# Q projection's last 64 rows in 32-row tiles, inside a 32-row transposition session

## The chip, the core and the metric

The kernel runs on one core of one Trainium2 chip. The metric is the device time of one execution in microseconds (us); the time shown for a kernel is the median of several runs. Engines are named as in the profile: PE (TensorE, matmuls; PEld are its weight loads), DVE (VectorE), ACT (ScalarE), POOL (GpSimd) and SP (SyncE, which issues nearly all DMAs here).

## The reference

Two independent attention blocks, A and B, of the same shape; their outputs are joined along the last axis. All arrays are bfloat16.

```python
# x (16, 80, 576); k_cache, v_cache (16, 16, 512, 128); wq (576, 4096); wo (4096, 576)
q = (x @ wq).reshape(16, 80, 32, 128).transpose(0, 2, 1, 3)
k = repeat(k_cache, 2, axis=1); v = repeat(v_cache, 2, axis=1)    # 16 kv heads, 32 q heads
p = softmax(einsum("bhqd,bhkd->bhqk", q, k) * 128 ** -0.5)
o = einsum("bhqk,bhkd->bhqd", p, v)
out = o.transpose(0, 2, 1, 3).reshape(16, 80, 4096) @ wo            # for A and for B
```

## The kernel before

**Units.** The work is cut into 128 units, 64 for A and then 64 for B. A unit is one batch and four kv heads, that is eight q heads. Each kv head has two q heads of 80 rows, 160 score rows: 128 of them fill one score tile (128 x 512), and the remaining 32 rows of the four kv heads make a fifth tile together. So a unit has five score tiles. Eight units (eight batches, the same heads) make an octet; Q is projected once for an octet.

**The steps of a unit, and their lines.**
- Q projection (L568). For each of the octet's eight heads, `em_qp` multiplies the head's 128 columns of wq by xT, over 576 contraction rows in five chunks of 128; the fifth chunk holds 64 rows of wq and 64 rows of zeros (set once by POOL, L400). It does so for the batches in two pieces, two batches (160 columns) and six batches (480 columns), each into one PSUM bank. `em_qev` evicts with the scale into `qT` (L579 on ACT, L580 on DVE).
- Scores. `em_qkr` (L672) makes the fifth tile of one or two units with four 32-column tiles of the array; `em_qk` (L686) makes each of the other four with one matmul of 512 columns.
- Softmax. DVE takes the negative row maximum (L695), ACT the exponential with the row sum (L699), DVE the reciprocal (L705), and POOL scales the probabilities in place (L708).
- Transposition (L741). `em_tr` turns the five scaled tiles into `pT`, with is-transpose matmuls against an identity. It uses 64-row tiles of the array, two at a time: 40 matmuls of 64 columns, into three banks. DVE copies two of the banks (L760, 1024 elements each), ACT or DVE the third (L758, L760).
- PV (L778): 16 matmuls of 160 columns, evicted to `oT` by ACT (L794).
- Output projection (L828): eight heads a step, 288 columns, over 16 heads; half of the sum waits in `acc` (L843), and the other half is added by DVE (L859) and stored.

```python
for n_ in range(20):                                                        # em_tr, before
    if n_ == 16:
        e.wait_ge(sems["e_tr"], U + 1)
    for h in range(2):
        ...
        last = e.matmul(dst, lhsT=p_sb[64 * h:64 * h + 64, psls[k_], j * 128:(j + 1) * 128],   # L741
                        rhs=ident[64 * h:64 * h + 64, 64 * h:64 * h + 64], start=True, stop=True,
                        is_transpose=True, tile_position=(64 * h, 0))
```

**Order.** Every operation is added to a list with a due time, a duration and the streams it belongs to. `_Sched.arrange` runs a planner over that list: it gives each operation its place on its engine, picks the PSUM bank among those that the operation's class allows (`BANKS`), and picks DVE or ACT where both are allowed. `finalize` then derives the semaphore waits from what each operation reads and writes. Each engine executes its list strictly in order. The planner treats score sessions of 32-column tiles (mode 1), transposition sessions (mode 2) and full-array matmuls (mode 0) as three modes and charges for a change between them.

**Loads.** SP loads K with a transposing DMA (five buffers) and V (four buffers), wq an octet at a time, wo in pieces, and for block B x with two transposing DMAs per half (512 rows, and 128 rows with the last 64). For block A, PE transposes x (L492).

## Time and profile before

| | |
|---|---|
| median of 3 runs | 739.65 us (738.3 to 740.1) |
| profiled execution | 739.38 us, its span 737.6 us |
| granted PE clock | 1.00 |
| POOL L708 | 640 instructions, 431.4 us busy |
| ACT L699 | 640, 443.1 us |
| DVE L695 | 640, 416.2 us |
| PE L568 / L778 / L686 / L828 / L741 | 1280 / 2048 / 512 / 1280 / 5120 matmuls |

"Busy" is the time in which an engine had at least one instruction under way; matmuls overlap, so that PE's busy time and the mean duration of a matmul say less than the distance from one start to the next. A line of the timeline gives the start in us, the time from the first start to the last end, the engine, the line of the kernel, the operation, what it writes and reads, and how many instructions were merged. "idle before" names what ended the wait.

### The profile page before, as it was taken

To read this page: it belongs to the slowest core of one execution; us is meant where nothing else is said; L and a number is where in the kernel's file an instruction comes from. 1 tells how busy PE (TensorE), PEld (TensorE's weight loads), DVE (VectorE), ACT (ScalarE), POOL (GpSimd) and SP (SyncE) were. 2 spreads that over 40 slices of the span, in tenths; PEclk is the share of its full clock that TensorE was granted. 3 is DMA by queue.
4 is the path that set the end of the run, shared out by engine and by line. 5 is a ranking of instruction groups with operands and counts; after the bars stand their busy time and mean duration, and the time that the engine had idled before them with its cause. 6 is when DMAs were issued, how large, how long until landed. Compare 5 with 4: busy or idle time off the path is not lost.

```text
span 737.6 us, 26159 instructions
## 1 busy us (share of the span) xinstructions
PE 730.7 (99%) x10818; PEld 510.8 (69%) x10818; DVE 650.3 (88%) x1344; ACT 625.7 (85%) x1827; POOL 433.8 (59%) x647
## 2 busy tenths in 40 slices
PE   9999999999999999999999999999999999999998
PEld 5566677677667676677677677666777677667776
DVE  4989999998999999888999999998889888998983
ACT  1889999999989889878889888989899888898881
POOL 1465666665666576556666565575565565665660
DMA  9999999999999999999999889999988978999920
GB/s 263 217 281 229 262 227 252 227 223 211 200 224 213 210 237 268 228 239 226 213 234 228 196 185 275 261 273 228 198 188 192 203 169 173 295 235 217 198 94 29
DMA packets 362102, 160.85 MB, mean 218 GB/s; under 512 B 276096, under 2 KB 358528, under 8 KB 361984
## 3 DMA queue, kind: packets, MB, share of 16 engines
q1 hardware_dynamic: 360768, 158.00, 97.3%
q8 instruction: 85, 1.39, 0.8%
q10 hardware_dynamic: 1216, 1.18, 0.5%
q14 instruction: 33, 0.27, 0.1%
HBM read 87.46 MB, written 2.95 MB: 123 GB/s over the span
## 4 chain that ended last, share of the span: by engine, by line
PE 96%; DVE 2%; ACT 1%; ACTq 0%; issue 0%
PE ps L568 23%; PE ps L828 21%; PE ps L778 19%; PE ps L686 15%; PE ps L741 12%; PE ps L672 5%; DVE negmax L695 1%; ACT p_sb L699 1%; PE ps L492 0%; DVE qT L580 0%; PE ps L429 0%; ACTq L545 0%; ACT oT L794 0%; ACT L448 0%; DVE pT L760 0%
## 5 line engine op out<-in xcount | busy, mean ns | idle before, releaser
L708 POOL TENSOR_SCALAR p_sb<-p_sb,rinv 128x512 bf16<-128x512 bf16 x640 | 431.4, 692 | 285.4 <-DVE rinv L705 283.5
L699 ACT ACTIVATE p_sb<-ps,negmax 128x512 bf16<-128x512 f32 x640 | 443.1, 701 | 27.8 <-DVE negmax L695 24.2
L695 DVE TENSOR_REDUCE negmax<-ps 128x1 f32<-128x512 f32 x640 | 416.2, 679 | 32.6 <-PE ps L672 16.8
L568 PE MATMUL ps<-xT,wq_sb 128*128 128x160 bf16 (+1 forms) x1280 | 206.0, 300 | 1.0 <-DVE xT L496 0.6
L778 PE MATMUL ps<-pT,v_sb 128*128 128x160 bf16 x2048 | 189.4, 233 | 0.0
L686 PE MATMUL ps<-kT,qT 128*128 128x512 bf16 x512 | 185.7, 380 | 0.0
L828 PE MATMUL ps<-wo_sb,oT 128*128 128x288 bf16 x1280 | 180.5, 286 | 0.0
L778 PEld LDWEIGHTS ps<-pT,v_sb 128*128 128x128 bf16 x2048 | 155.0, 98 | 35.1 <-DVE pT L760 0.6
L760 DVE COPY pT<-ps 128x1024 bf16<-128x1024 bf16 (+1 forms) x260 | 172.1, 676 | 6.0 <-PE ps L741 5.1
L568 PEld LDWEIGHTS ps<-xT,wq_sb 128*128 128x128 bf16 x1280 | 106.5, 98 | 66.1 <-issue 1.7
L828 PEld LDWEIGHTS ps<-wo_sb,oT 128*128 128x128 bf16 x1280 | 122.5, 98 | 40.6 <-issue 2.1
L699 ACT ACTIVATION_READ_ACCUMULATOR p_sb<-ps,negmax 128x1 f32 x640 | 137.5, 215 | 0.0
L794 ACT CAST oT<-ps 128x320 bf16<-128x320 f32 x256 | 108.7, 430 | 15.0 <-PE ps L778 14.1
L741 PEld LDWEIGHTS ps<-ident,p_sb 64*128 64x128 bf16 x5120 | 81.8, 95 | 37.9 <-issue 9.9
L741 PE MATMUL ps<-ident,p_sb 64*128 64x64 bf16 x5120 | 96.9, 190 | 0.0
L580 DVE TENSOR_SCALAR qT<-ps 128x480 bf16<-128x480 f32 (+1 forms) x131 | 65.2, 500 | 15.6 <-PE ps L568 14.7
L758 ACT COPY pT<-ps 128x256 f32<-128x256 f32 x124 | 47.3, 381 | 36.0 <-PE ps L741 35.4
L579 ACT ACTIVATE qT<-ps 128x160 bf16<-128x160 f32 (+1 forms) x125 | 52.8, 443 | 15.0 <-PE ps L568 14.3
L686 PEld LDWEIGHTS ps<-kT,qT 128*128 128x128 bf16 x512 | 49.6, 98 | 21.7 <-ACT p_sb L699 2.4
L705 DVE RECIPROCAL rinv<-rowsum 128x3 f32<-128x3 f32 (+1 forms) x256 | 41.2, 161 | 8.2 <-ACT p_sb L699 7.8
L672 PE MATMUL ps<-kT,qT 128*32 128x512 bf16 x512 | 39.6, 384 | 1.6 <-ACT p_sb L699 1.6
L859 DVE TENSOR_TENSOR osb<-ps,acc 128x288 bf16<-128x288 f32 x40 | 18.0, 451 | 16.1 <-PE ps L828 15.5
(25 smaller groups left out, 48.6 us busy)
## 6 DMA issues: line engine op xcount, KB each, us to landing
v_sb<-in_A_v_cache_dram SPq DMA_DIRECT2D x64, 512.0 KB, 4.8
v_sb<-in_B_v_cache_dram SPq DMA_DIRECT2D x64, 512.0 KB, 4.6
wo_sb<-in_A_wo_dram SPq DMA_DIRECT2D x8, 576.0 KB, 6.9
wo_sb<-in_B_wo_dram SPq DMA_DIRECT2D x8, 576.0 KB, 6.2
wq_sb<-in_B_wq_dram SPq DMA_DIRECT2D x4, 1024.0 KB, 7.1
out_dram<-osb SPq DMA_DIRECT2D x40, 72.0 KB, 3.7
wq_sb<-in_A_wq_dram SPq DMA_DIRECT2D x2, 1024.0 KB, 6.7
wq_sb<-in_A_wq_dram ACTq DMA_DIRECT2D x2, 512.0 KB, 6.9
```

The lines of the kernel that those rows point to most:

```text
L568: last = e.matmul(ps[:, vb.phys, 0:n1 - n0], lhsT=wq_sb[:, wsl, ck, i * 128:(i + 1) * 128], rhs=xT[:, half, ck, n0:n1], start=(ck == 0), s ...
L580: return e.tensor_scalar(dst, src, SCALE, None, op0=AluOpType.mult)
L672: last = e.matmul(ps[32 * g4:32 * g4 + 32, vb_.phys, :], lhsT=qT[:, qsl_, bl_, g4 * 160 + 128:g4 * 160 + 160], rhs=kT[:, ks_, :, g4 * 128: ...
L686: return e.matmul(ps[:, vb.phys, :], lhsT=qT[:, qsl, bl, gl * 160:gl * 160 + 128], rhs=kT[:, ks, :, gl * 128:(gl + 1) * 128], start=True, ...
L695: return e.tensor_reduce(negmax[:, si:si + 1], ps[:, vb.phys, :], axis=AX.X, op=AluOpType.max, negate=True)
L699: return e.activation(p_sb[:, psl, :], ps[:, vb.phys, :], AF.Exp, bias=negmax[:, si:si + 1], scale=1.0, accum_out=rowsum[:, ss, k:k + 1])
L708: return e.tensor_scalar(p_sb[:, psl, :], p_sb[:, psl, :], rinv[:, ss, k:k + 1], 1.0, op0=AluOpType.mult, op1=AluOpType.mult)
L741: last = e.matmul(dst, lhsT=p_sb[64 * h:64 * h + 64, psls[k_], j * 128:(j + 1) * 128], rhs=ident[64 * h:64 * h + 64, 64 * h:64 * h + 64], ...
L760: return e.tensor_copy(dst, src.rearrange("p (n c) -> p n c", n=16))
L778: last = e.matmul(ps[:, vo.phys, off:off + 160], lhsT=v_sb[:, vs, gl, j * 128:(j + 1) * 128], rhs=pT[:, pts, 4 * gl + j, :], start=(j == 0 ...
L794: return e.copy(dst, src)
L828: last = e.matmul(ps[:, vb.phys, 0:DC], lhsT=oT[:, hi, rb * 128:(rb + 1) * 128], rhs=wo_sb[:, wi, c3 * DC:(c3 + 1) * DC], start=(hi == 0), ...
```

## The change

**Q projection.** Work is cut into one piece per unit: two batches and four heads. Its first 512 rows are 16 full-array matmuls of 160 columns (four heads, four chunks). Each head has its own bank, and takes columns 320 to 479 of it. The last 64 rows become two rounds of four matmuls in 32-row tiles: round `h2` takes rows 32 `h2` to 32 `h2` + 31 for four heads at once, head r in the array's row group r. For that `wt` holds the last 64 rows of wq, 32 rows of each head on its own 32 partitions, and `xt` holds x's last 64 rows four times over. POOL makes the copies (`rep4`), and PE transposes them.

**Transposition.** 80 is-transpose matmuls of 32 columns in 32-row tiles, four at a time, into columns 0 to 319 (fp32) of the same four banks. Directly ahead of them, in the same session, come the eight tail matmuls of a later unit's Q. For 115 of the 128 pieces that is so; the 13 earliest have their tail among the other Q matmuls.

**Evictions.** The four banks are evicted two and two: DVE takes one pair, ACT the other (the table can swap them), with two copies each; the Q part follows (320 elements for two heads). PV evictions (`em_oev`) and the first half of the output projection (`em_ea`) may now be on either engine.

**Order.** The planner, its durations and `BANKS` go. `ORDER` is a string: each letter names a stream whose next operation is taken, an apostrophe ahead of it puts it on the other engine, and digits behind it are its banks.

**Sizes.** `NQ` (qT buffers) 3 to 2, `LA` (how far scores run ahead, in tiles) 10 to 11, `NS` (row maxima kept) 16 to 32; a small computation at the start (L439 to L451), whose result scales one accumulator copy (L841), goes. Wq of the first octet arrives in four pieces of 256 columns; the tail weights come in four loads for each set of eight heads.

```diff
@@ Q projection
-            for i in range(8):
-                for c in range(2):
...
-                        for ck in range(5):
-                            last = e.matmul(ps[:, vb.phys, 0:n1 - n0],
-                                            lhsT=wq_sb[:, wsl, ck, i * 128:(i + 1) * 128],
-                                            rhs=xT[:, half, ck, n0:n1], start=(ck == 0), stop=(ck == 4))
+            for m in range(8):
+                bp, hq = divmod(m, 2)
...
+                us = u0 - LQ + m
+                pre = us < US0
...
+                    def em_qp(e, h=h, hq=hq, wsl=wsl, half=half, n0=n0, vbq=vbq):
+                        for r in (2 * h, 2 * h + 1):
+                            for ck in range(4):
+                                last = e.matmul(ps[:, vbq[r].phys, QO:QO + 160],
+                                                lhsT=wq_sb[:, wsl, ck, (4 * hq + r) * 128:(4 * hq + r + 1) * 128],
+                                                rhs=xT[:, half, ck, n0:n0 + 160], start=(ck == 0), stop=False)
...
+                def em_qt(e, hq=hq, wsl=wsl, half=half, n0=n0, vbq=vbq):
+                    for h2 in range(2):
+                        for r in range(4):
+                            last = e.matmul(ps[:, vbq[r].phys, QO:QO + 160],
+                                            lhsT=wt[32 * r:32 * r + 32, wsl, h2, hq, :],
+                                            rhs=xt[32 * r:32 * r + 32, half, h2, n0:n0 + 160],
+                                            start=False, stop=(h2 == 1), tile_position=(32 * r, 0))
@@ transposition
-                    for h in range(2):
...
-                        last = e.matmul(dst, lhsT=p_sb[64 * h:64 * h + 64, psls[k_], j * 128:(j + 1) * 128],
-                                        rhs=ident[64 * h:64 * h + 64, 64 * h:64 * h + 64], start=True, stop=True,
-                                        is_transpose=True, tile_position=(64 * h, 0))
+                if td:
+                    td["emit"](e)
                 for n_ in range(20):
+                    k_, j = divmod(n_, 4)
+                    for r in range(4):
+                        last = e.matmul(psb[:, vts[r].phys, n_ * 32:n_ * 32 + 32],
+                                        lhsT=p_sb[32 * r:32 * r + 32, psls[k_], j * 128:(j + 1) * 128],
+                                        rhs=ident[32 * r:32 * r + 32, 32 * r:32 * r + 32], start=True, stop=True,
+                                        is_transpose=True, tile_position=(32 * r, 0))
@@ eviction of the transposition
-                    src = psb[:, vt.phys, 0:512] if h == 2 else psb[:, vt.phys, :]
-                    return e.tensor_copy(dst, src.rearrange("p (n c) -> p n c", n=16))
+                    f(pf[:, :, 64 * h // w:(64 * h + 64) // w].rearrange("p n (r c) -> p r n c", r=2),
+                      sf[:, a:b + 1:b - a, 128 // w:640 // w].rearrange("p r (n c) -> p r n c", n=16))
+                    return f(pf[:, 8 * h:8 * h + 8, 128 // w:160 // w].rearrange("p (r j) c -> p r j c", r=2),
+                             sf[:, a:b + 1:b - a, 0:128 // w].rearrange("p r (j c) -> p r j c", j=4))
@@ order
+        lines = dict((c, iter(streams[n])) for c, n in zip(LETTERS, sorted(streams)))
+        table = iter("".join(ORDER.split()))
+        for c in table:
+            other = c == "'"
+            op = next(lines[next(table) if other else c])
+            if op.alt:
+                op.eng = op.alt[other]
+            for vb in op.alloc:
+                vb.phys = int(next(table))
```

## The prediction

> **What bounds the kernel now.** I read the page first: busy shares and the chain that ended last.

> ```profile
> PE 730.7 (99%) x10818; PEld 510.8 (69%) x10818; DVE 650.3 (88%) x1344; ACT 625.7 (85%) x1827; POOL 433.8 (59%) x647
> ...
> PE 96%; DVE 2%; ACT 1%; ACTq 0%; issue 0%
> PE ps L568 23%; PE ps L828 21%; PE ps L778 19%; PE ps L686 15%; PE ps L741 12%; PE ps L672 5%; DVE negmax L695 1%; ACT p_sb L699 1%; PE ps L492 0%; DVE qT L580 0%; PE ps L429 0%; ACTq L545 0%; ACT oT L794 0%; ACT L448 0%; DVE pT L760 0%
> ```

> The chain lies on PE, and the two lines that the change rewrites (L568, Q projection; L741, transposition) hold 35% of it. Busy PE time overlaps itself, so I took the pace of each kind of matmul from the PE timeline, from one start to the next.

> ```profile
> 300.47 0.38 PE L686 MATMUL ps<-kT,qT 128*128 128x512 bf16 x1
> 300.79 0.76 PE L741 MATMUL ps<-ident,p_sb 64*128 64x64 bf16 x40
> 301.48 0.39 PE L686 MATMUL ps<-kT,qT 128*128 128x512 bf16 x1
> 301.70 0.51 PE L568 MATMUL ps<-xT,wq_sb 128*128 128x160 bf16 x5
> 302.05 0.38 PE L686 MATMUL ps<-kT,qT 128*128 128x512 bf16 x1
> 302.26 1.19 PE L568 MATMUL ps<-xT,wq_sb 128*128 128x480 bf16 x5
> 303.29 0.38 PE L686 MATMUL ps<-kT,qT 128*128 128x512 bf16 x1
> ...
> 50.25 1.27 PE L778 MATMUL ps<-pT,v_sb 128*128 128x160 bf16 x16
> ...
> 725.11 9.96 PE L828 MATMUL ps<-wo_sb,oT 128*128 128x288 bf16 x80
> ```

> Read to the nanosecond, the starts give these paces: 160 columns 69.2 ns (five from 301.70 to 302.05), 480 columns 202.6, 512 columns 215.8, 288 columns 122.6 (9.96 less one duration of 0.29, over 79). Columns at 2.4 per ns plus 2.5 ns gives all four. In the transposition session a pair (64-row tiles, the second 3.6 ns after the first) starts every 29.2 ns, which is 64 columns by the same formula. The session is framed by gaps: 0.311 us from the start of the 512-column matmul to it instead of 0.216, 0.122 instead of 0.029 behind it, and 11 ns more behind each first start (40 for 29, 80 for 69). So each change of tile shape costs about 95 + 11 = 106 ns, and PE makes 333 of them.

> Sum of before: Q 640 x (69.2 + 202.6) = 174.0; scores 512 x 215.8 + 128 x 215.8 = 138.1 (L686, L672); transposition 128 x 20 x 29.2 = 74.8; PV 2048 x 69.2 = 141.7; output 1280 x 122.6 = 156.9; shape changes 333 x 0.106 = 35.3; warm-up and x transposes 8; about 729 of a span of 737.6. The rest is the 5 us before the first real matmul and four idle stretches of 3.1 us in all. So PE is full almost end to end, and what leaves its stream leaves the time, until another engine or a wait takes its place.

> **The change, part by part.** The sum is made against the profiled execution, 739.4 us (span 737.6 and 1.8 around it); the median of the runs is 739.65.

> *Q projection, first 512 rows.* 1280 matmuls go (5 chunks of 160 and of 480 columns); 2048 of 160 columns come (16 per unit of two batches and four heads, 128 units): 2048 x 69.2 = 141.7. **-32.3.** The fifth chunk, half of it zeros, is what goes.

> *Its last 64 rows.* 8 matmuls per unit, in 32-row tiles, two rounds of four. If four run at once as the two of L741 do, a unit costs 2 x 69.2 ns, and 7 ns for the wider stagger: 128 x 0.145 = **+18.6.** If they ran one by one, 8 x 69.2: 70.9, which is 52 more.

> *Transposition in 32-row tiles.* 40 matmuls of 64 columns become 80 of 32 columns, 20 rounds of four. Per round: at least 32/2.4 + 2.5 = 15.8 ns, if the formula holds to 32 columns. Issue does not forbid it: in L672 a weight load and its matmul, with the next load and matmul, follow 3.3 ns apart, so four pairs need 13.2. At most, by the nearest row, the 29.2 ns of the pair, if that pace is set by what the trace can't separate from streaming (a load precedes its matmul by 28 ns there). 128 x 20 rounds: 40.4 to 74.8. No matmul in the trace is shorter than 64 columns, and the loads keep their 128 columns, so I take a value on the side of the measured row: 24 ns, 61.4. **-13.4** (bounds -34.4 and 0).

> [...]

> *Shape changes.* The tail shares the session's frame. But 13 early units have a tail session of their own, and fewer score sessions (L672) touch a transposition (41 for 53). Counted through the changed stream: 371 for 333. 38 x 0.106 = **+4.0.**

> *x.* 80 transposes of 128 columns for 50, 56 ns each: **+1.7.** Their replication is six POOL copies; a 512-element POOL instruction takes 0.69 us here, so some 6 us, in POOL's 285 us of idle time.

> *Other engines, by pace.* DVE: a reduction every 0.60 us, a 1024-element transposition copy 0.60, 512 elements 0.33, 160 and 480 elements of Q 0.23 and 0.57. Before: 382 + 153 + 41 + 14 + 20 + 14 + 5 = 629. After, 124 copies of 1024 and of 256 (0.60 + 0.20), 98 Q evictions of 320 (0.40), 114 PV evictions (0.40) and 24 output copies (0.37) make 99 + 39 + 46 + 9, with the rest 615. ACT the same way: 581, then 602 (132 pairs of copies at 0.61, 158 Q evictions at 0.32, 142 PV evictions). Both stay at 87% of what is left, DVE's share of before, so they cover nothing less than before. I add **+2** for new waits (0 to 10): four banks are now held from the first Q matmul of a unit to the last eviction, 1.1 + 0.6 + 1.2 us of about 5.6.

> *At nothing:* 32 small loads of the tail weights replace 8 loads, and two plain x loads replace two transposing ones, on SP: its issue stream waits over 550 us for buffers to come free, which hides them; were that cover gone, 32 at some 0.5 us would cost 16. A session's waits now stand ahead of its tail: behind them every PE instruction queues, as behind the old session's; what they wait for, POOL's scaling of five tiles, is an engine 59% busy. The third qT buffer goes, but a unit's Q, written per pair of batches, replaces one whose last reader (scores run 2.2 units ahead) is some six units back. The table also fixes which engine evicts; DVE's and ACT's sums above are counted with that.

> Sum: 739.4 - 32.3 + 18.6 - 13.4 + 4.0 + 1.7 + 2 = **720.0.** With the round at 15.8 and no new wait: 697; at 29.2: 733.

> **Rivals.**
> (1) *The transposition gains nothing*: loads set the pace and a round takes about 29 ns, 733. For it: loads of the same row group never follow faster than 29 ns in a steady session; against it: the first two follow by 15 ns. Chance 0.12.
> (2) *Evacuation*: with 87% busy evictors and four banks held by a unit, a Q matmul waits behind one DVE reduction (0.60 us) in every second unit: 64 x 0.60 = 38, 758. For it: eight banks, of which one unit holds half. Against it: before shows 92% DVE in 100 to 200 us and no idle PE. It decides from 0.15 us per unit (19.4/128); below that the change still gains. Chance 0.10. This is my slower case.
> (3) *Weight loads of different row groups one by one*: 29.2 ns for two loads could be 14.6 each; then 80 take 1.17 us a unit, 128 x (1.17 - 0.48) = 88 above mine, 808. Against it: loads of the two groups start 3.5 ns apart. Slower from 32 ns a round. Chance 0.05.
> (4) *The tail is not concurrent* (the change does not do what it says): 52 more, 772. Against it: two tiles and, in L672, four column tiles do run together. Chance 0.03.

> **Numbers.** The forecast, 720 (a round between 16 and 28 ns, few waits), has 0.70. The range reaches from 702 (18 ns, no wait) to 737, which takes in rival 1 with some waits and leaves out rivals 2 to 4, 0.18. A difference under 0.3% (2.2 us) can't be told from none. Faster: 0.70 and most of rival 1, 0.80; within 0.3%: the rest of it and mild forms of rival 2, 0.05; slower: 0.15.

> **What would show it.** Right: the start of the 80 transposes to the next matmul in about 0.6 us; the tail's 8 within 0.15 us ahead; Q matmuls 69 ns apart; PE still over 95% of the chain. Wrong: PE waits on ACT or DVE of over 10 us in all (rival 2), a session of 80 over 0.75 us (rival 1 at 0.70, rival 3 at 1.3), or a tail of 0.55 us (rival 4).

## The result, and the profile after

| | before | after |
|---|---|---|
| median | 739.88 us (738.3 to 741.06) | 797.62 us (789.82 to 805.35) |
| profiled execution | 739.38 us, span 737.6 | 805.35 us, span 803.6 |
| granted PE clock, mean | 1.000 | 0.987 |

The changed kernel is slower, by a ratio of 1.0747 (95% interval 1.0657 to 1.0837). The forecast was 720.0. The profiled execution is the longest of the four: the ratio leaves it out, and the parts below are summed against its 805.35 and not against the median. No trace shows how large the same parts were in the other three.

The page after, the lines that answer to those shown of before (busy time and instructions of each engine; the instruction queue's packets and megabytes; the chain that ended last):

```profile
PE 750.3 (93%) x17760; PEld 583.1 (73%) x17760; DVE 646.5 (80%) x1441; ACT 657.8 (82%) x1861; POOL 436.3 (54%) x652
...
q8 instruction: 140, 2.29, 1.2%
...
PE 87%; issue 6%; DVE 3%; ACT 3%; DMA 1%; SPq 0%
PE ps L810 20%; PE ps L761 18%; PE ps L541 17%; PE ps L673 14%; PE ps L721 10%; PE ps L660 4%; PE ps L556 4%; ACT p_sb L686 2%; DVE negmax L682 1%; DMA wt<-in_A_wq_dram 1%; DVE pT L739 1%; ACT pT L739 0%; DVE qT L571 0%; ACT qT L570 0%; SPq
```

DVE's busy time falls by 3.8 us and ACT's grows by 32.1 (from 650.3 and 625.7). What is new is the second entry of the chain: 6% "issue", time in which PE waited for nothing that the profile shows. Before, that entry was 0%. PE has 17,760 matmuls for 10,818, and the instruction queue moved 140 packets for 85, each of 16,384 bytes.

The waits of PE (what waited, what released it, microseconds in all, times, the longest) name the lines where that time lies:

```profile
PE ps L721 <- issue: 16.7, 17, 3.0
PE ps L761 <- issue: 15.3, 9, 3.3
PE ps L541 <- issue: 5.1, 4, 2.7
PE ps L810 <- issue: 3.6, 3, 2.5
PE ps L673 <- ACT p_sb L686: 1.5, 1, 1.5
```

Transposition, PV, Q projection and output projection all stop, the last although the change leaves its matmuls as they were. In this view "issue" comes to 40.7 us in 33 waits; all other waits listed come to 8.3. Before there was no "issue" among PE's waits, and the others came to 4.3, the longest two of them these:

```profile
PE ps L672 <- ACT p_sb L699: 1.6, 1, 1.6
PE ps L414 <- DVE ps L439: 1.2, 1, 1.2
```

One such stop on the timeline, in the middle of a PV step:

```profile
77.83 0.23 PE L761 MATMUL ps<-pT,v_sb 128*128 128x160 bf16 x1
81.34 0.24 PE L761 MATMUL ps<-pT,v_sb 128*128 128x160 bf16 x1 [3.27 <-issue]
81.46 0.38 PE L673 MATMUL ps<-kT,qT 128*128 128x512 bf16 x1
...
82.33 1.02 PE L541 MATMUL ps<-xT,wq_sb 128*128 128x160 bf16 x8
```

Two matmuls of one accumulation, whose operands are both there, lie 3.5 us apart.

**Where the stops lie in PE's program.** I counted PE's instructions (weight loads, matmuls, semaphore instructions) in the order of the trace. 35,818 of them in 140 packets are 256 to a packet. Of the gaps over 0.45 us with no semaphore behind them, the large ones resume at positions 193 to 195 modulo 256: a fixed place in each packet's worth of instructions. Counted there, as the distance from one matmul's start to the next less the shortest tenth of the same kind of pair, 47 stops cost 52.2 us. (The 40.7 of the view is less because it counts only idle time from the modelled end of a matmul.) Beside them I set the landings of the instruction packets from the trace's transfer records:

```
instruction packet     PE resumes at the next border
starts    lands        us, and how long it had stopped
65.05     65.93        67.54 (3.1)
71.32     72.26        73.58 (1.6)
78.73     79.88        81.34 (3.5)
84.15     85.07        87.93 (no stop at the border)
```

PE resumes 1.3 to 1.6 us after a packet's landing. Over the 140 blocks, a packet starts 2.2 us (median; 3.7 in the slowest tenth) after PE has passed the border before it and moves for 1.1 us; at the stops of over 0.45 us the next block begins 1.2 to 1.7 us after the landing, for which I take 1.3. That makes an estimated 4.6 us for a block of 256 instructions, 6.1 in the slowest tenth. The median block lasted 8.3 us before, so the packet was nearly always there in time (1.1 us of stops); after, it lasts 5.6. The stops are thus a race between the array and the supply of its own program.

**What follows a stop.** The windows view (busy time and instructions of PE, PEld, DVE, ACT and POOL, then granted clock, DMA share, GB/s) of two stretches behind the stop at 81.34:

```profile
81.30:83.30 2.00, 1.70 (x12) 1.27 (x13) 1.43 (x3) 1.68 (x6) 0.00 (x0) 0.82 1.03 244
83.30:85.30 2.00, 2.00 (x15) 1.19 (x16) 0.95 (x3) 2.00 (x8) 0.00 (x0) 0.50 0.49 170
```

The clock in the last stretch is 0.50, and the timeline line at 82.33 above has 8 matmuls of 160 columns in 1.02 us, which takes 0.72 elsewhere. The clock records hold six such stretches of 3.41 us in this execution and none in before. Matmuls in them ran 10.0 us behind their usual pace. This is the 0.987.

**The session.** The tail and the transposition on the timeline:

```profile
300.09 0.32 PE L556 MATMUL ps<-xt,wt 32*128 32x160 bf16 x8
300.24 0.80 PE L721 MATMUL ps<-ident,p_sb 32*128 32x32 bf16 x80
301.05 0.61 PE L660 MATMUL ps<-kT,qT 128*32 128x512 bf16 x8
```

The tail starts 0.15 us ahead of the transposition, as forecast. From the first transpose to the next matmul it is 0.81 us here. To the nanosecond (median of all sessions), rounds of four start 25 ns apart up to the seventh, and from there 33.4 ns apart, with single matmuls evenly 8.35 ns from one to the next. The 80 starts span 616 ns (before, 40 starts: 567). 128 sessions at 625 ns make 80.0 us against the 61.4 of the forecast.

### The profile page after: what moved, and what is told of

Read it like the earlier page. It is cut to its first block, busy times and chain, and to the rows that moved or that the text cites. A ratio compares the mean times of both kernels' runs of the same rounds, so it can differ in the third digit from the quotient of the medians.

```text
span 803.6 us, 40196 instructions
## 1 busy us (share of the span) xinstructions
PE 750.3 (93%) x17760; PEld 583.1 (73%) x17760; DVE 646.5 (80%) x1441; ACT 657.8 (82%) x1861; POOL 436.3 (54%) x652
## 4 chain that ended last, share of the span: by engine, by line
PE 87%; issue 6%; DVE 3%; ACT 3%; DMA 1%; SPq 0%
PE ps L810 20%; PE ps L761 18%; PE ps L541 17%; PE ps L673 14%; PE ps L721 10%; PE ps L660 4%; PE ps L556 4%; ACT p_sb L686 2%; DVE negmax L682 1%; DMA wt<-in_A_wq_dram 1%; DVE pT L739 1%; ACT pT L739 0%; DVE qT L571 0%; ACT qT L570 0%; SPq L510 0%
## 5 line engine op out<-in xcount | busy, mean ns | idle before, releaser
L695 POOL TENSOR_SCALAR p_sb<-p_sb,rinv 128x512 bf16<-128x512 bf16 x640 | 430.5, 692 | 346.0 <-DVE rinv L692 345.8
L686 ACT ACTIVATE p_sb<-ps,negmax 128x512 bf16<-128x512 f32 x640 | 438.1, 694 | 55.3 <-DVE negmax L682 44.2
L541 PE MATMUL ps<-xT,wq_sb 128*128 128x160 bf16 x2048 | 179.0, 234 | 6.1 <-issue 5.1
L541 PEld LDWEIGHTS ps<-xT,wq_sb 128*128 128x128 bf16 x2048 | 150.5, 99 | 30.8 <-issue 6.4
L739 DVE COPY pT<-ps 128x1024 bf16<-128x1024 bf16 x124 | 85.5, 690 | 68.5 <-PE ps L721 65.8
L686 ACT ACTIVATION_READ_ACCUMULATOR p_sb<-ps,negmax 128x1 f32 x640 | 133.4, 208 | 0.0
L721 PE MATMUL ps<-ident,p_sb 32*128 32x32 bf16 x10240 | 105.7, 177 | 16.9 <-issue 16.7
L721 PEld LDWEIGHTS ps<-ident,p_sb 32*128 32x128 bf16 x10240 | 98.8, 91 | 22.7 <-issue 19.9
L739 ACT COPY pT<-ps 128x512 f32<-128x512 f32 x132 | 77.5, 588 | 35.8 <-PE ps L721 34.0
L775 ACT CAST oT<-ps 128x320 bf16<-128x320 f32 x142 | 60.4, 431 | 24.6 <-PE ps L761 23.8
L570 ACT ACTIVATE qT<-ps 128x320 bf16<-128x320 f32 x158 | 66.5, 444 | 15.4 <-PE ps L556 8.9
L775 DVE CAST oT<-ps 128x320 bf16<-128x320 f32 x114 | 54.6, 481 | 8.2 <-PE ps L761 7.6
L571 DVE TENSOR_SCALAR qT<-ps 128x320 bf16<-128x320 f32 x98 | 46.8, 483 | 5.7 <-PE ps L556 3.3
```

Source lines behind the costliest of these rows:

```text
L541: last = e.matmul(ps[:, vbq[r].phys, QO:QO + 160], lhsT=wq_sb[:, wsl, ck, (4 * hq + r) * 128:(4 * hq + r + 1) * 128], rhs=xT[:, half, ck, ...
L686: return e.activation(p_sb[:, psl, :], ps[:, vb.phys, :], AF.Exp, bias=negmax[:, si:si + 1], scale=1.0, accum_out=rowsum[:, ss, k:k + 1])
L695: return e.tensor_scalar(p_sb[:, psl, :], p_sb[:, psl, :], rinv[:, ss, k:k + 1], 1.0, op0=AluOpType.mult, op1=AluOpType.mult)
L721: last = e.matmul(psb[:, vts[r].phys, n_ * 32:n_ * 32 + 32], lhsT=p_sb[32 * r:32 * r + 32, psls[k_], j * 128:(j + 1) * 128], rhs=ident[32 ...
L739: f(pf[:, :, 64 * h // w:(64 * h + 64) // w].rearrange("p n (r c) -> p r n c", r=2), sf[:, a:b + 1:b - a, 128 // w:640 // w].rearrange("p ...
L775: return (e.copy if en == "act" else e.tensor_copy)(dst, src)
```

## The experiments

Each was timed beside the kernel before, and the ratios are to that kernel's time then. The three columns on the right are of the profiled execution, in us. "Stops at block borders", "half clock" and "other waits" are counted as above from the trace, from 12 us on; two score matmuls in a row come at two regular paces (216 and 226 ns in both kernels) and are left out of the waits.

| kernel | us | stops at block borders | half clock | other waits |
|---|---|---|---|---|
| before | 739.9 | 1.1 | 0 | 4.7 |
| after | 797.6 (profiled 805.35) | 52.2 | 10.0 | 14.0 |
| 1: transposition in 64-row tiles | 754.1 | 3.7 | 1.6 | 12.8 |
| 2: and the tail in 64-row tiles | 747.2 | 0.9 | 3.9 | 20.9 |
| 3: after, K and V not loaded | 755.0 | 9.0 | 1.8 | 13.4 |
| 4: before, in shorter matmuls | 788.3 | 32.8 | 9.6 | 1.9 |
| 5: after, three row groups of four | 767.6 | 30.1 | 10.0 | 15.0 |
| 6: 2 in another order | 742.4 | 2.6 | 3.9 | 12.8 |

**1 and 2: fewer instructions, the rest of the change kept.** The theory (A) is that the supply of instructions stops PE. The rival (B) is that the new order, the four held banks and the evacuation (the evictions) do, whatever the number of instructions.

```diff
-                    for r in range(4):
-                        last = e.matmul(psb[:, vts[r].phys, n_ * 32:n_ * 32 + 32],
-                                        lhsT=p_sb[32 * r:32 * r + 32, psls[k_], j * 128:(j + 1) * 128],
...
+                    for h in range(2):
...
+                        last = e.matmul(dst, lhsT=p_sb[64 * h:64 * h + 64, psls[k_], j * 128:(j + 1) * 128],
+                                        rhs=ident[64 * h:64 * h + 64, 64 * h:64 * h + 64], start=True, stop=True,
```

> The changed kernel with its transpositions back in 64-row tiles (40 matmuls of 64 columns, in the same four banks; the tail stays in 32-row tiles; order, banks, evictions and waits as in the changed kernel). 12,640 matmuls for 17,760. Theory A (PE is short of instructions: its stalls lie where a new block of its instruction stream begins, and the 32-column rounds run at the sequencer's pace): my sum without new waits, 718.0, plus 13.4 (a round at 29.2 ns again) plus 12.2 (115 more changes of tile shape inside a session, 0.106 us each) = 744, and 0 to 6 of stalls: 744 to 750. Rival B (the new order with its four held banks makes PE wait for evictions): the stalls stay, about 795 to 805.

Measured: 754.14 us, ratio 1.0191 (1.0174 to 1.0209). The second takes the tail into 64-row tiles too, so that the session has one shape:

```diff
-                    for h2 in range(2):
-                        for r in range(4):
...
-                                            lhsT=wt[32 * r:32 * r + 32, wsl, h2, hq, :],
-                                            rhs=xt[32 * r:32 * r + 32, half, h2, n0:n0 + 160],
...
+                    for r in (0, 2, 1, 3):
+                        g_ = 64 * (r // 2)
...
+                                        lhsT=wt[g_:g_ + 64, wsl, r % 2, hq, :],
+                                        rhs=xt[g_:g_ + 64, half, 0, n0:n0 + 160],
```

> As before, and the tail in 64-row tiles too: two heads at once on 64 rows each, 4 matmuls a unit for 8, so that the whole session has one tile shape. 12,108 matmuls. Theory A: 718.0 + 13.4, less 2 for the smaller stagger and 20 fewer transposes of x = 729, and 0 to 6 of stalls: 729 to 736, faster than both. Rival B: 785 to 800.

Measured: 747.15 us, 1.0103 (1.0086 to 1.0121). Both are slower than theory A had them, by 4 us and by 11, and far below theory B. Order, banks and evacuation are those of the changed kernel, and the stops are gone, 52.2 to 3.7 and 0.9 us. What A had left out is the last column: PE's waits for other engines and loads. The waits view of the second:

```profile
PE ps L762 <- DMA v_sb<-in_A_v_cache_dram: 2.5, 2, 2.0
PE ps L656 <- ACT p_sb L682: 2.1, 2, 1.3
PE ps L552 <- DMA wt<-in_A_wq_dram: 1.9, 1, 1.9
```

These are transfers and evacuations that come late. That they do so because the order was made for other durations is a guess, which experiment 6 tries.

**3: the same instructions, less traffic.** The changed kernel with all 17,760 matmuls, but from the ninth unit on K and V are loaded as 64 elements each, so that it computes from old tiles.

```diff
+                if U >= 8:
+                    return e.dma_start(kT[0:1, ks, 0, 0:64], kc_ap[b, 4 * q, 0:1, 0:64])
...
+                if U >= 8:
+                    return e.dma_start(v_sb[0:1, vs, 0, 0:64], vc_ap[b, 4 * q, 0:1, 0:64])
```

> The changed kernel with the K and V loads from unit 8 on cut to 64 elements each; the scores and outputs of those units are computed from stale K and V. PE's instructions and the order are the same. Theory A1 (a block of instructions comes late because its DMA queues behind the K and V traffic): the stalls at block borders fall from 53 us to under 5, and the lower clock with them: 735 to 745. A2 (the block comes late whatever else moves): stays at 785 to 800. Rival B (evictions): 785 to 800.

Measured: 755.0 us, 1.0206 (1.0190 to 1.0221). That is 10 us above theory A1's range, and the stops fell to 9.0 us, not under 5; it is 30 us below A2 and B. A1 had left out what the other columns and the transposition cost. The page (instruction queue, chain) and the waits view:

```profile
q8 instruction: 140, 2.29, 1.3%
...
PE 90%; ACT 4%; DVE 3%; issue 1%; DMA 1%; SPq 0%
```

```profile
PE ps L725 <- issue: 4.7, 4, 2.5
PE ps L541 <- DVE negmax L686: 1.3, 1, 1.3
```

The same 140 packets, and "issue" falls from 6% to 1%. Per packet: the start behind the border goes from a median of 2.2 us to 0.9 and from 3.7 to 1.9 in the slowest tenth, with the packet's own 1.1 us hardly changed. So most of the lateness of the instruction packets comes from the K and V traffic; 0.9 us of it stays. 805.35 less the differences in the three columns (43.2, 8.2 and 0.6) is 753.4; the profiled execution took 754.3.

**4: the old kernel, with more instructions.** Nothing of the change: before's order, banks and tiles. The same columns are only cut into shorter matmuls, 17,218 for 10,818.

```diff
-                            last = e.matmul(ps[:, vb.phys, 0:n1 - n0],
...
+                        for m0 in range(n0, n1, 160):
...
+                                last = e.matmul(ps[:, vb.phys, m0 - n0:m0 - n0 + 160],
...
-                        return e.matmul(ps[:, vb.phys, :], lhsT=qT[:, qsl, bl, gl * 160:gl * 160 + 128],
-                                        rhs=kT[:, ks, :, gl * 128:(gl + 1) * 128], start=True, stop=True)
+                        for j in range(4):
+                            last = e.matmul(ps[:, vb.phys, j * 128:(j + 1) * 128], lhsT=qT[:, qsl, bl, gl * 160:gl * 160 + 128],
...
+                        for c in (0, 80):
+                            for j in range(4):
+                                last = e.matmul(ps[:, vo.phys, off + c:off + c + 80],
```

> The kernel before, with the same work in more and shorter matmuls: Q's 480 columns as 3 x 160, scores' 512 as 4 x 128, PV's 160 as 2 x 80; nothing else changed. 17,218 matmuls, about as many as the changed kernel's 17,760. By the paces of the trace the array needs 3.2 + 3.8 + 0.9 + 4.9 = 13 us more. Theory A: 752 and stalls at block borders on top, 10 to 40 us: 762 to 792. Rival B: 752, no stall.

Measured: 788.33 us, 1.0632 (1.0568 to 1.0695), inside theory A's range. The page and the waits view:

```profile
q8 instruction: 135, 2.21, 1.2%
...
PE 94%; issue 3%; DVE 2%; ACTq 0%; ACT 0%
```

```profile
PE ps L783 <- issue: 13.3, 8, 3.1
PE ps L745 <- issue: 7.0, 6, 2.9
```

The stops are there, 32.8 us of them at the block borders, without 32-row tiles, without held banks and without the new table. Before's 739.4, 13 for the array's own pace in shorter matmuls, and the differences in the three columns (31.7, 9.6, -2.8) make 790.9; the profiled execution took 791.8. With 3 this settles the supply of instructions as the main cause.

**5: what sets 33.4 ns.** Either the sequencer needs 8.35 ns for a load and its matmul (A), or the array and its four banks set the round (B). The fourth row group's transposes are left out.

```diff
-                    for r in range(4):
+                    for r in range(3):
```

> The changed kernel with the fourth 32-row group left out of every transposition session: 60 transposes of 32 rows instead of 80, and the last quarter of the probabilities' rows is filled with a copy of the third quarter, so the output is not attention. 15,200 matmuls instead of 17,760. In the changed kernel a session's rounds start 25 ns apart at first and 33.4 ns apart from about the seventh on, four matmuls 8.35 ns apart. Theory A (from there the sequencer's own pace of one load-and-multiply pair per 8.35 ns sets the round): three pairs need 25 ns, so the rounds stay at 25 to 26 ns from first to last, and the 60 starts of a session take 0.49 to 0.52 us instead of 0.62. Theory B (the array or the four banks they write set the later rounds): the later rounds stay near 33 ns, and a session takes 0.60 to 0.62 us. By A, 128 sessions shorten by some 14 us, and with 2,560 matmuls fewer part of the 52 us of stalls at borders of instruction blocks goes too: 755 to 780 us. By B: 780 to 800 us.

Measured: 767.55 us, one run, inside theory A's range. A session on its timeline:

```profile
303.78 0.32 PE L556 MATMUL ps<-xt,wt 32*128 32x160 bf16 x8
303.93 0.66 PE L721 MATMUL ps<-ident,p_sb 32*128 32x32 bf16 x60
304.52 0.73 PE L763 MATMUL ps<-pT,v_sb 128*128 128x160 bf16 x8
```

All rounds start 25 ns apart, to the last, and the 60 starts span 486 ns (median of 128). That is as A had it: a round of three takes three times 8.35 ns, a round of four four times, so nothing holds a round at a fixed 33 ns. A step of the array that takes 8.35 ns for each matmul would give the same; against it stand the first six rounds of the full session, four matmuls each in 25 ns. Which part of PE sets the 8.35 ns is not shown beyond that. Sessions shorter by 128 x 0.130 = 16.6 and stops shorter by 22.1 take 805.35 to 766.7.

**6: the rest.** Experiment 2's operations in another order and other banks, each engine's stream arranged anew; only `ORDER` differs.

> The kernel of the second experiment (Q projection's last 64 rows and transposes in 64-row tiles, 12,108 matmuls) with another order and other banks in its table: the same operations, none added, each engine's stream only arranged anew, and the choice between VectorE and ScalarE for the evacuations made anew. That kernel took 747.2 us, with some 22 us of waits of TensorE for other engines and transfers, against 3.6 in the kernel before, so without them it would stand near 729. Theory A (what is left of the loss in that kernel is the order and the banks: four banks held for a projection's tail, evacuations that come late): a better order takes back half of these waits or more, 734 to 742 us, and perhaps below the 739.8 of the kernel before. Theory B (the waits come from the engines' own load, 650 us of VectorE and 658 of ScalarE, and from four held banks in any order): the time stays at 745 to 752 us.

(The 22 and 3.6 us of waits in this expectation are 20.9 and 4.7 in the table's count.) Measured: 742.35 us, 1.0035 (1.0016 to 1.0054). The waits view:

```profile
PE ps L552 <- DMA wt<-in_A_wq_dram: 2.8, 1, 2.8
PE ps L410 <- DMA acc<-in_A_x_dram: 2.2, 1, 2.2
PE ps L762 <- issue: 1.4, 2, 1.2
PE ps L346 <- DVE wo_sb L339: 1.2, 1, 1.2
```

The last column falls from 20.9 to 12.8, so a part of these waits, 8.1 us, was the order's. That is less than the half that theory A asked for, and the time lies 0.35 us above its range, 0.35% above before; theory B's 745 to 752 is further off. No version here beats before. What remains, whether in the four held banks or in the order, is open; two long waits in this list, 5.0 us together, are early loads (at 11.9 and 32.9 us).

## Why the prediction was wrong

**Sum of before, Q main part and tail: right.** Q matmuls of 160 columns start 69 ns apart, the tail of 8 stands 0.15 us ahead of the transposes, as in "the start ... within 0.15 us". Rival 4 is out. The paces had DVE's work fall by 14 us and ACT's grow by 21; their busy times moved by -3.8 and +32.1, so each forecast was some 10 us too low. Two smaller slips changed nothing: 615 and 602 us of 720 are 85% and 84%, not 87%, and the idle stretches of 3.1 us in all are five, not four.

**A term was missing: the supply of PE's program.** The step that failed is "Issue does not forbid it". It looked at issue within one session only, by the spacing of four neighbours, and nothing in the sum or the rivals had a price for 6,942 more matmuls. The page of before had the line that was needed, its instruction queue with 85 packets:

```profile
q8 instruction: 85, 1.39, 0.8%
```

Over a span of 737.6 that is one packet per 8.7 us. With 17,760 matmuls on a sum of 720 it would have been one per 5.1 us. What before could not show is the price: with its 85 packets the stops came to 1.1 us. The runs give it for the profiled execution: +52.2 - 1.1 for the stops, and +10.0 for the six stretches of 3.41 us at half clock.

**The transposition: mechanism and size off.** "Four pairs need 13.2" took the 3.3 ns between four neighbours as a pace that lasts. It lasts for some six rounds; after that one load and matmul take 8.35 ns and a round 33.4. The term was -13.4 with bounds -34.4 and 0; it measured +5.2 (80.0 against 74.8), outside the bounds. The upper bound was the mistake here: it took "the 29.2 ns of the pair" as the worst case, which holds if the array or a row group sets the pace, but a round of four issues twice as many instructions as a round of two. The 24 ns of the forecast is close to the first rounds, at 25 ns. The prediction's own sign of "rival 1", a session over 0.75 us, appears at 0.81, by neither of the mechanisms given there: loads of one row group follow at 25 ns in the first rounds, and loads of different groups follow 8.35 ns apart in the later ones, not 14.6.

**New waits: +2 (0 to 10), measured +9.3** (14.0 against 4.7), within the range. Rival 2's mechanism is there in a mild form: PE's listed waits on ACT and DVE come to 7.1 us, under the 10 that were its sign, and it was neither the reason of the loss nor its 38 us. Experiment 6 shows that another order takes a part of such waits away, 8.1 of 20.9; how much of the rest is the four held banks' is open.

**The balance.** 720.0 less its 2 of waits is 718.0. With the session (+18.6), the stops (+51.1), the half clock (+10.0) and the waits (+9.3) that makes 807.0, for 805.35 profiled. By this sum, without the two causes that I had no row for, stops and clock, the change would still have stood at 746, slower than before, since the transposition costs 5.2 us where 13.4 were to be saved and the waits took 9.3.

**The range**, 702 to 737, held only cases in which PE's stream is limited by the array or by other engines. Rival 3, at 808 with a chance of 0.05, is nearest in time, but by luck: loads of different row groups follow 8.35 ns apart where it had 14.6, the sessions cost 18.6 us more than forecast where it had 88, and the time went elsewhere.

## What to carry to other kernels

Divide the span by the packets of the instruction queue before adding instructions to a full engine: here a block of 256 PE instructions needed an estimated 4.6 us, 6.1 in the slowest tenth, beside DMA traffic of 201 GB/s (mean), so 128 matmuls with their weight loads had to last about that long: 6.1 us over 128 is 48 ns a matmul. A pace read from a few neighbours need not last (here 25 ns a round up to the seventh, then 33.4); for a longer run of short matmuls take the pace at the end of the longest run in the trace, and when rows of the array are split further, bound the round by instructions too (8.35 ns for a load and its matmul here), not only by columns. A stop of PE can cost a second time, at half clock: 10.0 us here, beside 52.2 of stops.
